# Batches 1 to 7 of an attention-and-mixer kernel in blocks of 512 columns across the batch borders

## The chip, the cores and the metric

The kernel runs on one core of a Trainium2 chip. Its engines are TensorE (PE, with the weight load, PEld, counted apart), VectorE (DVE), ScalarE (ACT), GpSimd (POOL) and SyncE (SP), which here issues the DMA transfers. The metric is the device time of one execution in microseconds (us); three executions of the kernel before took 809.54, 811.75 and 812.27 us.

## The reference

There are 8 batches of 576 tokens, 8 heads and 64 dimensions per head. Attention runs within chunks of 64 tokens; then a mixer runs over tokens and over channels:

```python
scores = scale * np.matmul(q_c, k_c.transpose(0, 1, 2, 4, 3))      # chunks of 64
attn = softmax(scores); out = np.matmul(attn, v_c)                 # x: (8, 576, 512)
xt = x.transpose(0, 2, 1)
h = np.maximum(xt @ w_tok1, 0.0) @ w_tok2                          # 576 -> 256 -> 576
u = x + h.transpose(0, 2, 1)
h2 = np.maximum(u @ w_ch1, 0.0) @ w_ch2                            # 512 -> 1536 -> 512
return (u + h2).astype(np.float32)
```

All four mixer weights come in as float64 words. The token mixer (tok1, tok2) mixes the 576 tokens of one batch with each other; the channel mixer (ch1, ch2) treats every token alone, so for it the tokens of all batches are one row of 4608 columns.

## The kernel before

**Precision.** Each operand is split in a high part in fp32r and the rest in fp32r (names in `h` and `l`: `uh`, `ul`, `gh`, `gl`, `rh`, `rl`, `xh`, `xl`), and each product is three matmuls (the table `THREE`: high times high, low weight times high, high weight times low). In batch 0 tok1 and the plain products of tok2 work on fp32 instead.

**Weights.** A weight arrives as raw words (`raw_t` for the token mixer, `raw_c` for the channel mixer, L139, issued from SP in an order that the program gives). ACT (L156, L157), DVE (L160, L166, L173, L181) make fp32 of it, ACT (L225) its high part, DVE (L231) its low part. The 24 items of the channel mixer alternate: `c1_f` and `c2_f` for each f from 0 to 11. `AHEAD` says how many items ahead the load is issued; `convert(n)` takes n operations off the list of conversions, and the tables `FIRST_FILL`, `PREPARE`, `END_FILL` and `STEP_FILL` say how many at which place.

**Attention.** The 72 chunks of two batches make nine tiles of 128 tokens; the fifth is shared by both batches ("stack"). A tile goes through scores (QK, L270 and L309), maximum (L282), subtraction (L285), exponential (L289), a transpose through memory (DVE writes `blocks`, L332; SP writes `far`, L337, and reads it back as `pf`, L343; ACT copies `pt`, L360), the product with v (PV, L321 and L379), the scaling that gives `x` (L400), its split (`xh` by ACT L417, `xl` by POOL L418) and a second way through `far` into `xt`, the transposed x (L343). The shared tile goes through `xc` (SP, L429) and `xr` (ACT, L433) as well.

**Mixer.** Batch by batch. tok1 (L476) has two groups of 14 matmuls with 512 columns. ACT and DVE make `rh` (L493) and `rl` (L494) of them. tok2 (L514) works in two halves of 288 columns and four output parts m: eight groups of six matmuls of 288 columns, in the banks `ps_acc`; DVE adds `xt` (`u`, L519), ACT writes `uh` (L524), POOL or DVE writes `ul` (L525). Then, for each half, twelve steps f: ch1 (L535, 12 matmuls of 288 columns into one of two banks `ps_c1`), ACT writes `gh` (L544), DVE writes `gl` (L545), and one step later ch2 (L575, 12 matmuls into the four banks `ps_acc`). After the last step DVE and POOL add u (L582, L584) and SP stores 288 columns at a time. In batch 0, where the weights are still being converted, both halves go through ch1 together (the second half's g is kept), and the second half's ch2 runs at the end, beside the attention of batch 1. tok1 of the next batch stands round the last ch2 but one, and 28 attention steps are put at chosen steps f.

**What sets the order.** PE, ACT and DVE follow the written order until the first half of batch 0 has its u. After that the order of each engine comes from a scheduler that works with its own estimate of time; from batch 1 on, PE again follows the written order. Each engine works through its list in order, and SP does too: a DMA that waits for its data holds all that stand behind it.

## Time and profile before

| | |
|---|---|
| times of three executions, us | 809.54, 811.75, 812.27 (median 811.75) |
| span of the profiled execution, us | 808.2 |
| median less that span, us | 3.55 |
| PE busy in the span | 787.4 us (97%) |
| DVE, ACT, POOL busy | 378.0, 240.7, 118.5 us |
| mean granted TensorE clock | 0.992 |

The page gives the span of the profiled execution, from the first to the last instruction, and no time of its own; the timed executions have a median that is 3.55 us longer, which lies around the span. The profile has four stages: the start (0 to 43 us, attention of batch 0 and the first weights), batch 0 (43 to 152 us), batches 1 to 7 (152 to 804 us) and the last stores.

A row of the timeline has the start, the duration, the engine, the line, the operation and the tiles; "x2" stands for two equal instructions in a row, whose duration runs from the first start to the last end. Matmuls are pipelined, so the cost of one is read from start to start. "[2.49 <-ACT xh L417]" is idle time before the row and what ended it.

### The profile page before, as it was taken

Reading aid. Unit: us, or ns where it says so; the run is one execution under the profiler, and the core shown is the slowest. Engines: PE = TensorE matmul, PEld = TensorE weight load, DVE = VectorE, ACT = ScalarE, POOL = GpSimd, SP = SyncE. Lnnn points to the kernel's source line nnn. Section 1 sums busy time; section 2 is a strip of 40 time slices with the busy share of each in tenths; the row PEclk is TensorE's granted clock in tenths of the full one; section 3 lists DMA queues with packets and bytes.
Section 4 is the critical chain, followed back from the end, with each engine's and each line's share of the span. In section 5 each row is a group of like instructions: output and inputs, shape, how many; then the busy total and the mean of one; then the engine's idle time right before and its main releaser. Section 6 shows DMA issues by size and latency. Waiting matters only on the chain.

```text
span 808.2 us, 17939 instructions
## 1 busy us (share of the span) xinstructions
PE 787.4 (97%) x7556; PEld 752.1 (93%) x7556; DVE 378.0 (47%) x799; ACT 240.7 (30%) x496; POOL 118.5 (15%) x137
## 2 busy tenths in 40 slices
...
PEclk8999999999999999999999999999999999999999
...
GB/s 349 406 190 105 119 79 96 135 122 141 148 112 64 92 122 107 56 79 125 141 151 58 64 115 140 88 70 93 131 145 89 76 88 101 67 30 1 1 30 30
DMA packets 69985, 87.96 MB, mean 109 GB/s; under 512 B 8016, under 2 KB 48208, under 8 KB 69904
## 3 DMA queue, kind: packets, MB, share of 16 engines
...
q14 instruction: 22, 0.18, 0.1%
HBM read 59.92 MB, written 25.95 MB: 106 GB/s over the span
## 4 chain that ended last, share of the span: by engine, by line
PE 85%; DVE 8%; DMA 3%; ACT 2%; issue 1%; SPq 0%; ACTq 0%; DVEq 0%
PE acc L575 36%; PE ps_c L535 33%; PE ps_t L476 6%; PE ps_t L514 6%; PE ps_sv L309 2%; PE ps_sv L321 2%; DVE wtop L173 1%; DVE wtop L181 1%; DMA xc<-x 1%; DVE kept_c L231 1%; DVE wtop L160 1%; DMA raw_t<-in_w 1%; DMA pf<-far 1%; DVE wtop L166 1%; PE sum L485 0%
## 5 line engine op out<-in xcount | busy, mean ns | idle before, releaser
L535 PE MATMUL ps_c<-uh,kept_c 128*128 128x288 f32 x1536 | 310.8, 295 | 3.4 <-ACT xt L447 1.9
L575 PE MATMUL acc<-gh,kept_c 128*128 128x288 f32 x1536 | 311.9, 299 | 1.6 <-ACT kept_c L225 1.1
L535 PEld LDWEIGHTS ps_c<-uh,kept_c 128*128 128x128 f32 x1536 | 245.8, 188 | 4.8 <-ACT xt L447 2.1
L575 PEld LDWEIGHTS acc<-gh,kept_c 128*128 128x128 f32 x1536 | 244.2, 188 | 6.4 <-ACT kept_c L225 1.8
L535 PE MATMUL ps_c<-ul,kept_c 128*128 128x288 f32 x768 | 226.6, 295 | 0.0
L545 DVE SCALAR_TENSOR_TENSOR gl<-ps_c,gh 128x288 fp32r<-128x288 f32 x180 | 81.4, 452 | 310.1 <-ACT gh L544 309.9
L575 PE MATMUL acc<-gl,kept_c 128*128 128x288 f32 x768 | 219.5, 295 | 0.0
L544 ACT ACTIVATE gh<-ps_c 128x288 fp32r<-128x288 f32 x180 | 74.1, 411 | 317.1 <-PE ps_c L535 316.6
L535 PEld LDWEIGHTS ps_c<-ul,kept_c 128*128 128x128 f32 x768 | 144.2, 188 | 0.1
L575 PEld LDWEIGHTS acc<-gl,kept_c 128*128 128x128 f32 x768 | 142.9, 189 | 0.1
L418 POOL TENSOR_TENSOR xl<-x,xh 128x512 fp32r<-128x512 f32 x28 | 38.3, 1366 | 413.0 <-ACT xh L417 413.0
L584 POOL TENSOR_TENSOR o<-o,ul 128x288 f32<-128x288 f32 x56 | 44.1, 813 | 192.7 <-DVE o L582 191.1
L514 PE MATMUL ps_t<-kept_t,rh 128*128 128x288 f32 x224 | 44.7, 295 | 0.3 <-ACT rh L493 0.3
L289 ACT ACTIVATE pr<-pr 128x512 f32<-128x512 f32 x36 | 22.7, 632 | 61.6 <-DVE pr L285 59.9
L582 DVE TENSOR_TENSOR o<-acc,uh 128x288 f32<-128x288 f32 x56 | 22.7, 448 | 36.1 <-PE acc L575 31.5
L476 PE MATMUL ps_t<-xh,kept_t 128*128 128x512 f32 x112 | 36.0, 405 | 2.5 <-ACT xh L417 2.5
L524 ACT CAST uh<-u 128x288 fp32r<-128x288 f32 x64 | 27.1, 433 | 37.6 <-DVE u L519 37.6
L360 ACT COPY pt<-pf 128x512 f32<-128x512 f32 x31 | 19.2, 620 | 60.3 <-DMA pf<-far 60.3
L514 PEld LDWEIGHTS ps_t<-kept_t,rh 128*128 128x128 f32 x224 | 35.9, 188 | 1.0 <-ACT rh L493 1.0
L514 PE MATMUL ps_t<-kept_t,rl 128*128 128x288 f32 x112 | 33.2, 297 | 0.2 <-DVE rl L494 0.2
L519 DVE TENSOR_TENSOR u<-ps_t,xt 128x288 f32<-128x288 f32 x64 | 28.4, 452 | 9.8 <-PE ps_t L514 9.4
L525 POOL TENSOR_TENSOR ul<-u,uh 128x288 fp32r<-128x288 f32 x35 | 29.1, 848 | 10.0 <-ACT uh L524 9.5
...
## 6 DMA issues: line engine op xcount, KB each, us to landing
...
```

Source lines behind the costliest of these rows:

```text
L289: nc.scalar.activation(out=pr, in_=pr, func=AF.Exp, scale=1.0 / float(D) ** 0.5)
L418: nc.gpsimd.tensor_tensor(out=xl, in0=t["x"], in1=xh.bitcast(F32), op=ALU.subtract)
L476: nc.tensor.matmul(ps, lhsT=lhsT, rhs=rhs, start=(n == 0 and q == 0), stop=(n == len(mt) - 1 and q == len(terms) - 1),)
L514: nc.tensor.matmul(ps[:, :HALF], lhsT=lhsT[:, m * P:(m + 1) * P], rhs=rhs, start=(k == 0 and q == 0), stop=(k == NT1 - 1 and q == len(term ...
L519: nc.vector.tensor_tensor(out=u.rearrange("p (i c) -> p i c", c=BK), in0=ps[:, :HALF].rearrange("p (i c) -> p i c", c=BK), in1=xt[:, n * H ...
L524: nc.scalar.copy(out=uh[:, m], in_=u)
L525: return lambda engine: engine.tensor_tensor(out=ul[:, m], in0=u, in1=uh[:, m].bitcast(F32), op=ALU.subtract)
L535: nc.tensor.matmul(ps[:, :HALF], lhsT=weights["c1", f][:, wi, k * P:(k + 1) * P], rhs=u[ui][:, k], start=(k == 0 and q == 0), stop=(k == N ...
L544: nc.scalar.activation(out=gh, in_=ps[:, :HALF], func=AF.Relu)
L545: nc.vector.scalar_tensor_tensor(out=gl, in0=ps[:, :HALF], scalar=0.0, in1=gh.bitcast(F32), op0=ALU.max, op1=ALU.subtract)
L575: nc.tensor.matmul(accs[e], lhsT=weights["c2", f][:, wi, e * P:(e + 1) * P], rhs=g[gi], start=(f == 0 and q == 0), stop=(f == NFC - 1 and ...
L584: nc.gpsimd.tensor_tensor(out=o, in0=o, in1=u[1][:, e].bitcast(F32), op=ALU.add)
```

## The change

Batch 0 stays in two halves of 288 columns. The 4032 tokens of batches 1 to 7 become one row of columns, cut in seven blocks of 512 and one of 448. tok2 of a block is made in pieces cut at the batch borders: 512; 64+448; 128+384; 192+320; 256+256; 320+192; 384+128; 448. Each piece has four parts m of six matmuls. The function that writes it is `block_tok2`; its four groups go to the two banks `ps_c1` in turn and the fourth to the bank of the attention (`ps_at`), not to `ps_acc`. `turn(k + 1)` places them between ch2 of f = 10 and ch2 of f = 11 of the block before. tok1 of batch k + 2 (both groups) stands after ch1 of f = 11, ahead of ch2 of f = 10. The attention steps stand at f in `SLOTS`, every second step, and the first one is moved into batch 0.

`xt` is a buffer per block (two of them) beside one for batch 0; u, uh and ul are tiles of one part m; `ul` is written by POOL for m = 0 and 2 and by DVE for m = 1 and 3. The tok2 weights come in two items of 576 columns and not four of 288. `AHEAD` goes from 6 to 2 and the tables of fills are new. v is loaded with its column of ones for the first nine tiles alone. The output is laid out as 4 x 128 x 4608 and stored in pieces of 512 columns.

```diff
-AHEAD = 6
+N = 512
+BLOCKS = [(k * N, min(N, (B - 1) * S - k * N)) for k in range(-(-(B - 1) * S // N))]
+SLOTS = {0: (1, 3, 5, 7, 9), 1: (2, 4, 6, 8), 2: (1, 3, 5, 7, 9)}
+UL_ON_VECTOR = {1, 3}
+AHEAD = 2
...
-END_FILL = (4, 3, 1)
-STEP_FILL = (5, 5)
+END_FILL = (4, 3, 1, 1, 1, 3, 2)
+STEP_FILL = (4, 5, 5, 5, 5, 5, 5, 4, 5, 5, 5, 5, 5, 5, 5, 5, 5, 6, 5, 5, 5, 6, 5, 5)
...
-    plan += [(("t2", k, n), w2_in, k * S + n * HALF, HALF) for n in range(2) for k in range(NT1)]
+    plan += [(("t2", k), w2_in, k * S, S) for k in range(NT1)]
...
+    def block_tok2(k, rs, m, dst, ps):
+        uh, ul = dst
+        cols = slice(m * P, (m + 1) * P)
+        base, width = BLOCKS[k]
+        at = 0
+        while at < width:
+            b, lo = divmod(base + at, S)
+            n = min(S - lo, width - at)
+            terms = [
+                (rs[b + 1][t][ri], weights["t2", t][:, wi, lo:lo + n]) for t in range(NT1) for wi, ri in THREE
+            ]
+            for q, (lhsT, rhs) in enumerate(terms):
+                nc.tensor.matmul(
+                    ps[:, at:at + n], lhsT=lhsT[:, cols], rhs=rhs,
+                    start=(q == 0), stop=(q == len(terms) - 1),
+                )
+            at += n
+        u = pool.tile([P, N], F32, tag="o", name="u", bufs=8)[:, :width]
...
+            in1=block_x(k)[:, :width // BK, m], op=ALU.add,
+        )
+        nc.scalar.copy(out=uh[m], in_=u)
+        (nc.vector if m in UL_ON_VECTOR else nc.gpsimd).tensor_tensor(
+            out=ul[m], in0=u, in1=uh[m].bitcast(F32), op=ALU.subtract
+        )
...
+    def turn(k, rs):
+        u = block_u(BLOCKS[k][1])
+        for m in range(NDT):
+            if m < 3:
+                ps = ps_c1.tile([P, 512], F32, tag="c1", name="ps_t2")
+            else:
+                ps = ps_at.tile([P, 2, 512], F32, tag="at", name="ps_t2")[:, 0]
+            block_tok2(k, rs, m, u, ps)
+        return u
...
+        if f == NFC - 1:
+            after.close()
+            by_hand.enter_context(tc.manual_schedule(engines={nc.tensor.engine}))
+            u = turn(0, rs)
+        ch2(HALF, HALF, us[1], f, g, accs)
+        extras(2 * NFC + f)
+        if f == FIRST_QK:
+            attention(0)
+
+    done = 1
+    for k, (at, width) in enumerate(BLOCKS):
+        mixes = k + 2 if k + 2 < B else None
+        steps = SLOTS[0] if k == 0 else SLOTS[1 + (len(batch_tiles(mixes)) == 5)] if mixes else ()
...
+        for f in range(NFC):
+            g = ch1(u, f, width=width)
+            if f in steps:
+                attention(done)
+                done += 1
+            end = f == NFC - 1
+            if end and mixes:
+                rs[mixes] = [tok1(mixes, m) for m in range(NT1)]
+            if pend is not None:
+                ch2(*pend)
+            pend = (S + at, width, u, f, g, accs)
+            if end and k + 1 < len(BLOCKS):
+                u = turn(k + 1, rs)
+            if end:
+                ch2(*pend)
```

The order on PE at the border of batches 1 and 2, before: the last tok1 matmul (`stack` is the shared tile, `half_low` its masked low weights), ch2 of f = 11, then tok2 in groups of 288 columns, and ch1 of f = 0 at the end.

```order
L476 MATMUL ps_t1_3454<-stack_3290,half_low0_2053 128x512
L575 MATMUL acc_2979<-gh_3419,kept_c2_11_1687 128x288 x2
L575 MATMUL acc_2979<-gl_3420,kept_c2_11_1687 128x288
...
L514 MATMUL ps_t2_3503<-kept_t2_0_0_2076,rh_3438 128x288 x2
L514 MATMUL ps_t2_3503<-kept_t2_0_0_2076,rl_3439 128x288
L514 MATMUL ps_t2_3503<-kept_t2_1_0_2098,rh_3469 128x288 x2
L514 MATMUL ps_t2_3503<-kept_t2_1_0_2098,rl_3470 128x288
...
L535 MATMUL ps_c1_3597<-uh_3501,kept_c1_0_648 128x288 x2
```

The same place in the changed kernel, at the end of block 0, with its own line numbers (L504 is tok1, L572 tok2, L594 ch1, L636 ch2):

```order
L504 MATMUL ps_t1_2982<-stack_2888,half_low_2068 128x512
L636 MATMUL acc_2372<-gh_2930,kept_c2_10_1555 128x512 x2
...
L572 MATMUL ps_t2_3021<-kept_t2_0_2074,rh_2146 128x64 x2
L572 MATMUL ps_t2_3021<-kept_t2_0_2074,rl_2147 128x64
L572 MATMUL ps_t2_3021<-kept_t2_1_2112,rh_2181 128x64 x2
L572 MATMUL ps_t2_3021<-kept_t2_1_2112,rl_2182 128x64
L572 MATMUL ps_t2_3021<-kept_t2_0_2074,rh_2978 128x448 x2
...
L636 MATMUL acc_2372<-gh_2959,kept_c2_11_1609 128x512 x2
...
L594 MATMUL ps_c1_3122<-uh_3013,kept_c1_0_575 128x512 x2
```

ch1 and ch2 are 512 wide, tok2 moved ahead of ch2 of f = 11, and each of its groups here is a piece of 64 columns (the rest of batch 1) and one of 448 (batch 2).

The order on PE at the end of batch 0, before: the last ch2 rows, the last PV (L379), then the share of the last attention tile (`xh_1991`) in tok1, then tok2.

```order
L575 MATMUL acc_1897<-gl_2165,kept_c2_11_1687 128x288
L379 MATMUL ps_v_1953<-v_1597,pt_1951 64x65 x16
L476 MATMUL ps_t1_2145<-xh_1991,kept_t1_2_2_2028 128x512 x2
L476 MATMUL ps_t1_2180<-xh_1991,kept_t1_2_2_2028 128x512 x2
L476 MATMUL ps_t1_2145<-xl_1992,kept_t1_2_2_2028 128x512
L476 MATMUL ps_t1_2180<-xl_1992,kept_t1_2_2_2028 128x512
L514 MATMUL ps_t2_2239<-kept_t2_0_0_2076,rh_2160 128x288 x2
```

And in the changed kernel (L397 is PV, L327 QK, `xh_1951` the last tile's):

```order
L397 MATMUL ps_v_1913<-v_1572,pt_1911 64x65 x16
L636 MATMUL acc_1865<-gh_2115,kept_c2_10_1555 128x288 x2
...
L327 MATMUL ps_sv_1995<-qk_1766 64x64 x16
L504 MATMUL ps_t1_2131<-xh_1951,kept_t1_2_2_1992 128x512 x2
L504 MATMUL ps_t1_2166<-xh_1951,kept_t1_2_2_1992 128x512 x2
L504 MATMUL ps_t1_2131<-xl_1952,kept_t1_2_2_1992 128x512
L504 MATMUL ps_t1_2166<-xl_1952,kept_t1_2_2_1992 128x512
L572 MATMUL ps_t2_2195<-kept_t2_0_2074,rh_2146 128x512 x2
...
L636 MATMUL acc_1863<-gh_2150,kept_c2_11_1609 128x288 x2
```

Six matmuls of ch2 of f = 10 and the QK of the next tile now stand between the last PV and the tok1 rows that need it, and ch2 of f = 11 stands behind the four tok2 groups of block 0.

The order of the loads on SP in the first part of batch 0, before: `xc` behind the raws up to `c1_10`.

```order
L139 DMA raw_c2_7_117<-in_wc2 128x1024
L139 DMA raw_c1_9_113<-in_wc1 128x1024
L139 DMA raw_c2_8_109<-in_wc2 128x1024
L139 DMA raw_c1_10_105<-in_wc1 128x1024
L429 DMA xc_1158<-x_663 64x512
...
L139 DMA raw_c2_9_101<-in_wc2 128x1024
L139 DMA raw_c1_11_97<-in_wc1 128x1024
L139 DMA raw_c2_10_93<-in_wc2 128x1024
```

And in the changed kernel (L140 raws, L447 `xc`, L355 `far`, L361 its way back):

```order
L140 DMA raw_c2_7_117<-in_wc2 128x1024
L447 DMA xc_1131<-x_637 64x512
...
L140 DMA raw_c1_9_113<-in_wc1 128x1024
L140 DMA raw_c2_8_109<-in_wc2 128x1024
L140 DMA raw_c1_10_105<-in_wc1 128x1024
...
L140 DMA raw_c1_11_97<-in_wc1 128x1024
L355 DMA far_1422<-blocks_1420 128x512
L361 DMA pf_1424<-far_1422 32x4x128 x4
L140 DMA raw_c2_10_93<-in_wc2 128x1024
L140 DMA raw_c2_11_89<-in_wc2 128x1024
```

`xc` moved ahead of three raws, and the last two raws moved behind the reading back of the second tile's transpose.

On DVE, before, c2_10 is clamped (L160) side by side with c1_11 soon after the second tile's transpose (`blocks_1446`):

```order
L332 STREAM_TRANSPOSE blocks_1446<-pr_1399 128x4x4x32
L181 ISA wtop_1319<-wtop_1319,low_1320 128x1024
L160 TENSOR_SCALAR wtop_1432<-wtop_1432 128x512
...
L160 TENSOR_SCALAR wtop_1515<-wtop_1515 128x512
L181 ISA wtop_1432<-wtop_1432,low_1433 128x1024
L160 TENSOR_SCALAR wtop_1569<-wtop_1569 128x512
```

In the changed kernel (L166 is the clamp, L187 the add, L237 the low part; `wtop_1490` is c2_10):

```order
L350 STREAM_TRANSPOSE blocks_1420<-pr_1342 128x4x4x32
L187 ISA wtop_1292<-wtop_1292,low_1293 128x1024
L237 TENSOR_TENSOR kept_c1_9_1340<-wtop_1223,kept_c1_9_1340 128x512
...
L187 ISA wtop_1445<-wtop_1445,low_1446 128x1024
L237 TENSOR_TENSOR kept_c2_9_1457<-wtop_1406,kept_c2_9_1457 128x512
L411 TENSOR_SCALAR zi_1523<-ps_v_1506 128x8
L166 TENSOR_SCALAR wtop_1490<-wtop_1490 128x512
```

The clamp of c2_10 moved from the 14th to the 19th place behind the transpose, with 17 conversions and gl and one small `zi` (L411) between.

More of the change, by code (lines that the diff above doesn't have):

```diff
@@ L152, in words_scalar @@
         st = raws[i][1]
-        tag, bufs = (f"wt{n}", token) if i < token else ("wt", 4)
-        tops[i] = pool.tile([P, n], F32, tag=tag, name="wtop", bufs=bufs)
-        lows[i] = pool.tile([P, DM], I32, tag="low", name="low", bufs=3)[:, :n]
+        if i < token:
+            if "t" not in tops:
+                tops["t"] = pool.tile([P, sum(p[3] for p in plan[:token])], F32, tag="wtt", name="wtt", bufs=1)
+            lo = sum(p[3] for p in plan[:i])
+            tops[i] = tops["t"][:, lo:lo + n]
+        else:
+            tops[i] = pool.tile([P, n], F32, tag="wt", name="wtop", bufs=4)
+        lows[i] = pool.tile([P, max(n, DM)], I32, tag="low" if n < S else "low_t", name="low", bufs=3)[:, :n]
         nc.scalar.activation(out=tops[i], in_=st[:, :, 1].bitcast(F32), func=AF.Abs)
@@ L442, in attn_x @@
                 continue
+            if b:
+                first, end = ((b - 1) * S + j * P + r for r in (0, rows.stop - rows.start))
+                while first < end:
+                    k, at = divmod(first, N)
+                    n = min(end - first, N - at)
+                    part = slice(rows.start, rows.start + n)
+                    far_in(tiles[t]["x"], block_x(k)[:, at // BK:(at + n) // BK], part)
+                    rows = slice(part.stop, rows.stop)
+                    first += n
+                continue
             dst = xt[:, 4 * j:4 * j + (rows.stop - rows.start) // BK]
@@ L666, in attention_mixer_kernel @@
     second = batch_tiles(1)
+    order = [t for b in range(2, B) for t in batch_tiles(b)]
     attn_load(second[0])
```

210 lines of the change are left out of this document (95 added, 115 removed).

## The prediction

> **What bounds the kernel now.** I read the page first, then busy time by stretch, then the timelines of the two stretches where something is lost. The page, with the clock in tenths over the span and the chain that ended last:
>
> ```profile
> span 808.2 us, 17939 instructions
> PE 787.4 (97%) x7556; PEld 752.1 (93%) x7556; DVE 378.0 (47%) x799; ACT 240.7 (30%) x496; POOL 118.5 (15%) x137
> PEclk8999999999999999999999999999999999999999
> PE 85%; DVE 8%; DMA 3%; ACT 2%; issue 1%; SPq 0%; ACTq 0%; DVEq 0%
> ```
>
> PE is busy for 97% of the span. Busy time by stretch (us, number of instructions in brackets, then granted clock, DMA share, GB/s) says where the rest is:
>
> ```profile
> 43.00:60.00 17.00, 16.00 (x110) 13.35 (x110) 14.83 (x33) 10.91 (x21) 0.00 (x0) 0.90 0.45 164
> 60.00:80.00 20.00, 20.00 (x173) 19.31 (x172) 20.00 (x43) 15.20 (x30) 0.00 (x0) 1.00 0.31 106
> 80.00:100.00 20.00, 19.29 (x166) 18.19 (x165) 20.00 (x40) 14.43 (x28) 2.99 (x1) 1.00 0.37 120
> 100.00:120.00 20.00, 18.84 (x191) 17.76 (x190) 17.27 (x36) 9.87 (x21) 4.72 (x5) 1.00 0.21 68
> 143.80:152.00 8.20, 5.27 (x35) 3.64 (x27) 4.29 (x10) 1.73 (x4) 4.13 (x5) 0.79 0.28 92
> 230.00:700.00 470.00, 470.00 (x4611) 458.63 (x4610) 192.36 (x400) 116.34 (x242) 76.66 (x84) 1.00 0.31 98
> ```
>
> From 230 to 700 us PE never idles and has its full clock, so in batches 1 to 7 only fewer or shorter matmuls save time. From 60 to 100 DVE, converting weights, is full too: there PE and DVE bind together.
>
> **The wide matmuls.** The price of one, on PE's timeline:
>
> ```profile
> 700.48 0.42 PE L535 MATMUL ps_c<-uh,kept_c 128*128 128x288 f32 x2
> ...
> 710.02 0.42 PE L535 MATMUL ps_c<-uh,kept_c 128*128 128x288 f32 x2
> ...
> 711.60 0.39 PE L476 MATMUL ps_t<-stack,kept_t 128*128 128x512 f32 x1
> ...
> 714.86 0.42 PE L575 MATMUL acc<-gh,kept_c 128*128 128x288 f32 x2
> ```
>
> From 700.48 to 710.02 lie three steps of 24, so 9.54 / 72 = 132.5 ns for 288 columns. From 711.60 to 714.86 lie the 14 matmuls of one tok1 group: 232.9 ns for 512. The slope is 100.4 / 224 = 0.448 ns a column, and 3.4 ns are left that every matmul pays. ch1 and ch2 of batches 1 to 7 are 7 x 576 = 4032 matmuls of 288 now (534.2 us) and become 2016 of 512 (469.5) and 288 of 448 (204.2 each, 58.8): 528.3, a gain of 5.9. If ch2, which changes its bank every three matmuls, costs 1 ns more than tok1 at 512, 1.2 of that goes. I take **-5.0**, with 3 and 8 as the ends, which the last digit of the four rows allows. The number of columns stays, so nothing larger is to be had.
>
> The Trainium skill, "TensorE: Matmul & The Clock Gate", section "Back-to-back issue gap", gives N/2.4 + 2.5 ns for an isolated matmul, and 131 ns for N = 512 in a sustained stream. By the first the gain would be 1728 x 2.5 = 4.3 us; the second would make the stage 200 us shorter, and the 232.9 ns above, from a sustained stream, contradict it.
>
> **tok2 in pieces.** Batches 1 to 7 have 24 x 14 = 336 tok2 matmuls before and after, of the same 96768 columns. But 24 now have 64 columns, 48 have 128 and 48 have 192, which by the slope take 32, 61 and 89 ns. A weight load of 128 columns goes with each, and no row of 128-column weights in fp32r shows less than 132 ns. The nearest rows:
>
> ```profile
> 23.16 0.60 PE L351 MATMUL ps_x<-ident,x 128*128 128x128 f32 x4
> 23.60 0.60 PE L351 MATMUL ps_t<-ident,pr 128*128 128x128 f32 x4
> ...
> 266.78 0.69 PE L309 MATMUL ps_sv<-qk 64*64 64x64 f32 x32
> 267.29 0.65 PE L321 MATMUL ps_sv<-v,pt 64*64 64x64 f32 x32
> ```
>
> L351 takes 0.44 / 4 = 110 ns with 128 columns of fp32 and a load of 128. QK takes 0.51 / 32 = 16 ns in tiles of a quarter of the array, 64 ns for each quarter. A floor of 110 costs 24 x 78 + 48 x 49 + 48 x 21 ns = 5.2 us, one of 64 costs 0.9, none costs 0. I take **+2.0**, nearer to the small tiles, since L351's fp32 is not the type here.
>
> The Trainium skill, "TensorE: Matmul & The Clock Gate", section "LDWEIGHTS (loading the stationary operand)", has P/1.2 ns for P columns, 107 for 128. Were that the floor, the pieces would cost 4.9 us and the time would be 2.9 longer than my sum; no row before shows it.
>
> **The end of batch 0.** PE, DVE, ACT and SP there:
>
> ```profile
> 143.34 0.70 PE L379 MATMUL ps_v<-v,pt 64*64 64x65 f32 x32
> 146.53 2.08 PE L476 MATMUL ps_t<-xh,kept_t 128*128 128x512 f32 x4 [2.49 <-ACT xh L417]
> 148.40 1.06 PE L476 MATMUL ps_t<-xl,kept_t 128*128 128x512 f32 x2
> 149.72 0.55 PE L514 MATMUL ps_t<-kept_t,rh 128*128 128x288 f32 x2 [0.26 <-ACT rh L493]
> 150.44 0.40 PE L514 MATMUL ps_t<-kept_t,rl 128*128 128x288 f32 x1 [0.18 <-DVE rl L494]
> ...
> 151.28 0.43 PE L514 MATMUL ps_t<-kept_t,rh 128*128 128x288 f32 x2
> ...
> 143.11 1.55 DVE L582 TENSOR_TENSOR o<-acc,uh 128x288 f32<-128x288 f32 x4 [4.66 <-issue]
> ...
> 145.07 0.69 DVE L400 TENSOR_TENSOR x<-ps_v,zi 128x512 f32<-128x512 f32 x1
> ...
> 148.57 1.73 SPq L343 DMA_DIRECT2D xt<-far  x4
> ```
>
> The last PV ends at 144.04 (call that T); DVE is still at the four o adds, so x starts at T + 1.0, and PE waits 2.49 us. The matmuls behind the wait run at about half speed (the stretch's clock is 0.79). Up to 151.28 pass 7.24 us with 6 x 0.233 + 6 x 0.1325 = 2.2 of work: 5.0 lost. After the change the o adds come later, x starts at T + 0.5, and 0.8 us of ch2 and 0.5 of QK stand behind PV. xh's matmuls follow x's start by 1.46 as now, so at T + 2.0: a wait of 0.7. xl (POOL, 1.37 us a piece) comes another 0.5 late. rh and rl behind the shorter tok1 cost some 0.7. Then two tok2 groups of 1.4 run to T + 7.4, and the third needs the bank `ps_c1` of the first, which u (DVE) has to leave; u needs xt of the last tile. That lands now 6.5 us after x is ready (145.76 to 150.30 + 2.0), so at T + 7.7, and u takes 0.7: a new wait of 1.0. Loss after: 2.9. **-2.1**, with 0 and 5 as the ends. ch2 of f = 11 then gives 1.6 us for the last uh and ul.
>
> **Attention and its transfers.** One wait of batches 1 to 7 goes, and the transfer of the shared tile moves:
>
> ```profile
> PE ps_sv L321 <- ACT pt L360: 0.5, 1, 0.5
> PE ps_c L535 <- ACT uh L524: 1.0, 1, 1.0
> ...
> 276.63 0.62 ACT L360 COPY pt<-pf 128x512 f32<-128x512 f32 x1 [1.63 <-DMA pf<-far]
> ...
> 41.35 9.72 DMA xc<-x
> ...
> 51.10 0.62 ACT L433 CAST xr<-xc 64x512 fp32r<-64x512 f32 x1 [2.92 <-DMA xc<-x]
> ```
>
> From QK (266.78) to the end of pt is 10.5 us; steps will be two f apart, 48 x 0.233 = 11.2, with 1.1 of attention in them 12.3. So the 0.5 goes: **-0.5**. xc is issued at 41.35 and lands 9.72 us later behind the raws; ACT waits for it 2.92 us with uh queued behind, and PE 1.0 for uh. With three raws fewer ahead of it that ends: **-1.0**.
>
> The last two raws speak against the change. They will be issued behind the pf of the second tile:
>
> ```profile
> 94.71 0.33 SPq L337 DMA_DIRECT2D far<-blocks  x1
> 96.77 1.75 SPq L343 DMA_DIRECT2D pf<-far  x4
> DMA to landing us min/median/max: 5.1/5.7/6.9
> ...
> L231 DVE TENSOR_TENSOR kept_c<-wtop,kept_c 128x512 fp32r<-128x512 f32 x12 | 8.1, 674 | 0.0
> L545 DVE SCALAR_TENSOR_TENSOR gl<-ps_c,gh 128x288 fp32r<-128x288 f32 x7 | 3.1, 444 | 0.0
> ```
>
> The third row is that of raws (L139) issued from 60 to 100 us; the last two have DVE's mean ns of one in about that stretch. From the transpose to the end of the pf issues are 3.8 us, and with 0.4 for its own issue and 5.7 c2_10 lands after 9.9. In the new order DVE has 17 other conversions and gl between that transpose and c2_10's first operation: 11 of 0.67 us (sign, add, low part) and 6 of 0.44 (clamp, shift, gl), 10.0 us, of which ACT needs 0.7 for itself: 0.6 late, 1.8 at the slowest landing. ACT would stand at the raw with gh behind it. **+0.5**.
>
> At the start AHEAD, the fills and the wider tok2 items shift some 2 us of DVE work ahead of the first ch1 and take about as much out of the stretch where DVE is full: 0, with 2 each way. In a step of 5.6 us, gh and gl at 512 columns take what these do:
>
> ```profile
> L494 DVE SCALAR_TENSOR_TENSOR rl<-ps_t,rh 128x512 fp32r<-128x512 f32 x14 | 9.5, 686 | 21.1 <-ACT rh L493 21.1
> L493 ACT ACTIVATE rh<-ps_t 128x512 fp32r<-128x512 f32 x14 | 8.3, 597 | 45.3 <-PE ps_t L476 45.3
> ...
> 804.26 0.46 DVE o L582
> ```
>
> 0.6 and 0.7 us lie beside 2.8 us of ch2, so they cost nothing; were they bare, it would be 1.3 a step. The last add on 448 columns and its store: **+0.3**.
>
> **Sum.** -5.0 + 2.0 - 2.1 - 0.5 - 1.0 + 0.5 + 0.3 = -5.8, a span of 802.4. The median lies 3.55 above the span, so 806.0 against 811.75.
>
> **Rivals.** *Batch 0 gains more.* The stretches from 43 to 120 lose 1.0 + 0.7 + 1.2 in idle and 1.7 by the clock of 0.90; if the new fills end most of it (3.5 more), the end of batch 0 loses half of what I say (1.5) and the pieces have no floor (2.0), the time is 799. For it: DVE runs full from 60 us on, and what it has done earlier is no longer in the way; against: the conversions are as many as before, and PE idles little. *The pieces and turns eat the gain.* With a floor of 110 ns (+3.2) and 0.15 us of waiting at each of seven turns (+1.0) it is 810.2, within the noise of no change. *The attention chain becomes the bound, slower.* A step has 12.3 us, the chain 10.5 today. gh and gl in front of its six DVE and ACT operations, u and ul at the turns and SP's stores of 512 columns ahead of `far` can lengthen it; above 12.3 PE waits at PV in each of 28 steps. From 12.6 on (0.3 x 28 = 8.4) the change is slower; at 12.65, 806.0 + 9.8 = 815.8. Against it: DVE is busy for 192 of 470 us, and 1.8 us are in hand. *A long stream of 512 columns runs faster than the tok1 group*: every 10 ns would be 20 us. The group's 14 in a row at 232.9 show no such trend. The 131 ns of the Trainium skill ("TensorE: Matmul & The Clock Gate", "Back-to-back issue gap") would make it some 600 us.
>
> **How the numbers follow.** Chances: the forecast (802 to 809) 0.45, more in batch 0 (795 to 802) 0.22, gain eaten (809.3 to 814.2) 0.20, chain or another new wait (above 814.2) 0.12, the faster stream 0.01. A measurement of this kernel tells 0.3% from no change, 809.3 to 814.2. So faster 0.45 + 0.22 + 0.01 = 0.68, same 0.20, slower 0.12. The range from 797 to 813.5 leaves out some of the first rival and the slower one.
>
> **What would show it.** ch1 and ch2 at 232 to 234 ns from start to start in the new trace; the pieces of 64 and 128 columns at 32 and 61 ns (no floor) or near 110; PE's wait for xh at the end of batch 0 under 1 us and one for u or xt before the third tok2 group; no PE wait for pt; ACT's wait for xc gone, one for the last raws below 2 us. I am wrong if PE shows waits at the turns or at PV in each step, or if the first 150 us move by more than 5 us.

## The result and the profile after

The changed kernel takes 803.83 us (median of 803.06, 803.81, 804.65 and 803.84) against 812.01 for the kernel before in the same runs (809.54 to 812.36): a ratio of 0.9906, interval 0.9891 to 0.9921. That is 8.2 us faster; forecast were 806.0, and 797 to 813.5 as the range.

The profiled execution after took 803.06 us, 1.76 more than its span of 801.3. The page of the changed kernel, the same lines as before:

```profile
span 801.3 us, 14067 instructions
PE 781.5 (98%) x5828; PEld 650.2 (81%) x5828; DVE 364.9 (46%) x664; ACT 223.2 (28%) x394; POOL 108.7 (14%) x94
PEclk7999999999999999999999999999999999999999
PE 81%; DMA 9%; DVE 7%; issue 1%; SPq 1%; ACT 0%; POOL 0%; ACTq 0%; DVEq 0%
```

Busy time by stretch of the changed kernel (us, instructions in brackets, granted clock, DMA share, GB/s):

```profile
43.00:60.00 17.00, 14.36 (x105) 12.46 (x103) 16.74 (x38) 12.63 (x25) 0.00 (x0) 0.90 0.18 61
60.00:80.00 20.00, 19.44 (x172) 18.98 (x171) 19.22 (x41) 15.38 (x31) 0.00 (x0) 1.00 0.32 106
80.00:100.00 20.00, 20.00 (x179) 19.77 (x178) 20.00 (x41) 13.85 (x27) 2.49 (x1) 1.00 0.42 141
143.80:152.00 8.20, 6.76 (x54) 4.30 (x47) 5.93 (x11) 2.57 (x6) 1.98 (x2) 1.00 0.47 142
230.00:700.00 470.00, 470.00 (x3409) 386.59 (x3409) 186.01 (x311) 103.50 (x171) 74.37 (x56) 1.00 0.30 97
```

From 230 to 700 us PE is still busy all the time, now with 3409 matmuls and not 4611. PE's waits from 43 to 160 us in the changed kernel (us in total, times, longest); behind 160 us the view is empty, so no wait at any turn and none for `pt` in batches 1 to 7:

```profile
PE ps_v L397 <- ACT pt L378: 3.4, 3, 1.3
PE ps_c L594 <- ACT xt L475: 2.6, 1, 2.6
PE ps_t L572 <- DVE rl L522: 0.8, 1, 0.8
...
PE ps_t L572 <- ACT rh L521: 0.5, 1, 0.5
...
```

**Where the 6.9 us of span went.** From the start of the first tok2 of batch 1's tokens to the start of the last matmul (before 149.72 and 803.86, after 146.77 and 797.31) pass 654.14 us before and 650.55 after, with ch2 of batch 0's f = 11 (1.58 us) in the latter alone. I added up every matmul there from its start to the next one's:

| us, start to start | before | after | difference |
|---|---|---|---|
| ch1 and ch2 of batches 1 to 7 | 539.5 | 529.8 | -9.7 |
| tok2 | 45.1 | 51.2 | +6.1 |
| QK and PV | 30.4 | 29.0 | -1.4 |
| tok1 | 39.2 | 39.0 | -0.2 |
| ch2 of batch 0, f = 11 | | 1.6 | +1.6 |

Ahead of this stage the change wins 2.95 (149.72 to 146.77), behind it 0.4. The 2.95 is one execution against one: in four experiments below that have the same code up to the first tok2 (the halves, the half loads, the turns last, four matmuls a group) it starts at 145.23 to 148.33. From the last PV to the first tok2 pass 5.3 us in each of them, as here, against 6.4 before.

The wide matmuls on PE's timeline of the changed kernel, two pairs of rows, each one step of 24 matmuls apart:

```profile
300.48 0.61 PE L594 MATMUL ps_c<-uh,kept_c 128*128 128x512 f32 x2
306.05 0.63 PE L594 MATMUL ps_c<-uh,kept_c 128*128 128x512 f32 x2
...
719.87 0.62 PE L594 MATMUL ps_c<-uh,kept_c 128*128 128x512 f32 x2
725.40 0.63 PE L594 MATMUL ps_c<-uh,kept_c 128*128 128x512 f32 x2
```

5.57 / 24 = 232.1 and 5.53 / 24 = 230.4 ns for 512 columns. In the last block 448 take 204.5 in the mean.

The pieces of 64, 128 and 192 columns in the changed kernel, each with the row that follows the six matmuls of its group, and the two rows of the 448 columns behind the 64:

```profile
232.31 0.30 PE L572 MATMUL ps_t<-kept_t,rh 128*128 128x64 f32 x2
232.45 0.28 PE L572 MATMUL ps_t<-kept_t,rl 128*128 128x64 f32 x1
232.56 0.39 PE L572 MATMUL ps_t<-kept_t,rh 128*128 128x64 f32 x2
232.89 0.65 PE L572 MATMUL ps_t<-kept_t,rh 128*128 128x448 f32 x2
233.39 0.36 PE L572 MATMUL ps_t<-kept_t,rl 128*128 128x448 f32 x1
...
318.09 0.33 PE L572 MATMUL ps_t<-kept_t,rh 128*128 128x128 f32 x2
318.71 0.56 PE L572 MATMUL ps_t<-kept_t,rh 128*128 128x384 f32 x2
...
404.53 0.36 PE L572 MATMUL ps_t<-kept_t,rh 128*128 128x192 f32 x2
405.18 0.48 PE L572 MATMUL ps_t<-kept_t,rh 128*128 128x320 f32 x2
```

A group of six takes 0.58, 0.62 and 0.65 us, nearly the same for 64, 128 and 192 columns. Between the third and the fourth matmul of the 64 (232.45 to 232.56) lie 110 ns. Only the first of a group is shorter, since its load ran beside the wide matmul ahead of it; the wide piece behind pays some back (0.50 us for its first two).

The end of batch 0 in the changed kernel: PE from the last PV to the last group of tok2, and ch2 of f = 11 behind:

```profile
141.49 0.70 PE L397 MATMUL ps_v<-v,pt 64*64 64x65 f32 x32 [1.33 <-ACT pt L378]
...
144.19 1.19 PE L504 MATMUL ps_t<-xh,kept_t 128*128 128x512 f32 x4
146.77 0.73 PE L572 MATMUL ps_t<-kept_t,rh 128*128 128x512 f32 x2 [0.52 <-ACT rh L521]
149.28 0.50 PE L572 MATMUL ps_t<-kept_t,rl 128*128 128x512 f32 x1 [0.77 <-DVE rl L522]
153.78 0.42 PE L636 MATMUL acc<-gh,kept_c 128*128 128x288 f32 x2
```

The wait for xh (2.49 us before) is gone. PV ends at 142.12, where ch2 goes on. From there to 153.78 pass 11.66 us with 6 x 0.1325 of ch2, 0.5 of QK and 30 x 0.232 of tok1 and tok2, 8.3 of work: 3.4 lost, against 5.0 before. About half of it is in the waits shown, the rest in matmuls that run slower behind them (146.77 to 149.28).

### The profile page after: what moved, and what is told of

Same layout as the page of the kernel before. It is cut to its first block, busy times and chain, and to the rows that moved or that the text cites. A ratio compares the mean times of both kernels' runs of the same rounds, so it can differ in the third digit from the quotient of the medians.

```text
span 801.3 us, 14067 instructions
## 1 busy us (share of the span) xinstructions
PE 781.5 (98%) x5828; PEld 650.2 (81%) x5828; DVE 364.9 (46%) x664; ACT 223.2 (28%) x394; POOL 108.7 (14%) x94
## 4 chain that ended last, share of the span: by engine, by line
PE 81%; DMA 9%; DVE 7%; issue 1%; SPq 1%; ACT 0%; POOL 0%; ACTq 0%; DVEq 0%
PE acc L636 33%; PE ps_c L594 33%; PE ps_t L572 6%; PE ps_t L504 5%; DMA raw_c<-in_wc 3%; DMA far<-blocks 2%; PE ps_sv L327 2%; DMA raw_t<-in_w 2%; PE ps_sv L339 2%; DMA pf<-far 1%; DMA xc<-x 1%; DVE wtop L187 1%; DVE wtop L179 1%; DVE kept_c L237 1%; SPq L361 1%
## 5 line engine op out<-in xcount | busy, mean ns | idle before, releaser
L636 PE MATMUL acc<-gh,kept_c 128*128 128x512 f32 (+2 forms) x960 | 273.2, 374 | 0.0
L594 PE MATMUL ps_c<-uh,kept_c 128*128 128x512 f32 (+1 forms) x768 | 238.3, 391 | 0.0
L606 DVE SCALAR_TENSOR_TENSOR gl<-ps_c,gh 128x512 fp32r<-128x512 f32 (+2 forms) x108 | 70.9, 657 | 319.3 <-ACT gh L605 319.3
L636 PEld LDWEIGHTS acc<-gh,kept_c 128*128 128x128 f32 x960 | 170.3, 188 | 29.8
L636 PE MATMUL acc<-gl,kept_c 128*128 128x512 f32 (+2 forms) x480 | 170.7, 370 | 0.0
L594 PEld LDWEIGHTS ps_c<-uh,kept_c 128*128 128x128 f32 x768 | 144.1, 188 | 31.0
L594 PE MATMUL ps_c<-ul,kept_c 128*128 128x512 f32 (+1 forms) x384 | 149.8, 390 | 0.0
L605 ACT ACTIVATE gh<-ps_c 128x512 fp32r<-128x512 f32 (+2 forms) x108 | 61.6, 570 | 291.7 <-PE ps_c L594 291.6
L636 PEld LDWEIGHTS acc<-gl,kept_c 128*128 128x128 f32 x480 | 88.0, 188 | 15.0
L436 POOL TENSOR_TENSOR xl<-x,xh 128x512 fp32r<-128x512 f32 x28 | 37.5, 1338 | 375.4 <-ACT xh L435 364.4
L594 PEld LDWEIGHTS ps_c<-ul,kept_c 128*128 128x128 f32 x384 | 72.1, 188 | 15.7
L572 PE MATMUL ps_t<-kept_t,rh 128*128 128x448 f32 (+7 forms) x224 | 48.6, 311 | 0.5 <-ACT rh L521 0.5
L594 PE MATMUL ps_c<-both,kept_c 128*128 128x288 f32 x288 | 44.1, 304 | 3.2 <-ACT xt L475 2.6
L594 PEld LDWEIGHTS ps_c<-both,kept_c 128*128 128x128 f32 x288 | 40.4, 193 | 4.1 <-ACT xt L475 2.9
L572 PEld LDWEIGHTS ps_t<-kept_t,rh 128*128 128x128 f32 x224 | 37.3, 189 | 2.6 <-ACT rh L521 0.9
L572 PE MATMUL ps_t<-kept_t,rl 128*128 128x448 f32 (+7 forms) x112 | 34.9, 313 | 0.8 <-DVE rl L522 0.8
```

The lines of the kernel that those rows point to most:

```text
L436: nc.gpsimd.tensor_tensor(out=xl, in0=t["x"], in1=xh.bitcast(F32), op=ALU.subtract)
L572: nc.tensor.matmul(ps[:, at:at + n], lhsT=lhsT[:, cols], rhs=rhs, start=(q == 0), stop=(q == len(terms) - 1),)
L594: nc.tensor.matmul(ps[:, :width], lhsT=weights["c1", f][:, wi, k * P:(k + 1) * P], rhs=u[ui][k], start=(k == 0 and q == 0), stop=(k == NDT ...
L605: nc.scalar.activation(out=gh, in_=ps[:, :width], func=AF.Relu)
L606: nc.vector.scalar_tensor_tensor(out=gl, in0=ps[:, :width], scalar=0.0, in1=gh.bitcast(F32), op0=ALU.max, op1=ALU.subtract)
L636: nc.tensor.matmul(accs[e], lhsT=weights["c2", f][:, wi, e * P:(e + 1) * P], rhs=g[gi], start=(f == 0 and q == 0), stop=(f == NFC - 1 and ...
```

## The experiments

All of them start from the changed kernel; a ratio is against the kernel before in the same set of runs. Its median lay between 810.7 and 812.0 from set to set, so a microsecond between two versions says little.

**Is the gain the price of a matmul?** Every wide matmul of ch1 and ch2 but the first of its bank is made in two halves of 256:

```diff
-                nc.tensor.matmul(
-                    ps[:, :width], lhsT=..., rhs=u[ui][k],
-                    start=(k == 0 and q == 0), stop=(k == NDT - 1 and q == 2),
+                for lo, hi in HALVES(width, k == 0 and q == 0): nc.tensor.matmul(
+                    ps[:, lo:hi], lhsT=..., rhs=u[ui][k][:, lo:hi],
+                    start=(k == 0 and q == 0), stop=(k == NDT - 1 and q == 2 and hi == width),
```

> The changed kernel with the ch1 and ch2 matmuls of the seven 512-column blocks issued as two matmuls of 256 columns each (all but the first of each accumulation): 1904 more matmuls, the same columns, nothing else. The forecast's theory, 3.4 ns for every matmul beside its columns, expects 1904 x 3.4 = 6.5 us more, 810.3 us. The rival, that a wide matmul is cheaper than its tok1 row said and the fixed part larger (two of 256 at 118.2 ns against one of 512 at 230.9 in the changed kernel's trace, 5.5 ns), expects 10.5 us more, 814.3 us. If neither a fixed part nor anything else counts, 803.8 us.

It took 817.89 us (816.72 to 818.44), ratio 1.0086 [1.0061, 1.0112]: 14.1 more than the changed kernel for 1904 more matmuls, 7.4 ns each, above both expectations. Its waits up to 160 us are those of the changed kernel to within 0.1 us. One step on its PE timeline, 47 matmuls, one of them whole:

```profile
733.10 0.64 PE L594 MATMUL ps_c<-uh,kept_c 128*128 128x512 f32 x3
738.82 0.64 PE L594 MATMUL ps_c<-uh,kept_c 128*128 128x512 f32 x3
```

(5.72 - 0.23) / 46 = 119.3 ns for 256 columns, so two of them cost 7.6 more than one of 231. Fewer matmuls for the same columns are what the change gains in this stage, and a matmul more at 256 columns costs over twice the 3.4 ns that I had read from two widths. It brings a weight load of its own; the run doesn't tell the two apart.

**What holds the narrow pieces up?** Four of the six matmuls of a piece below 256 columns load 64 weight columns and not 128 (so half of the output rows lack these four products):

```diff
+ROWS = lambda n, q: P if n >= 256 or q in (0, 3 * NT1 - 1) else P // 2
...
-                    ps[:, at:at + n], lhsT=lhsT[:, cols], rhs=rhs,
+                    ps[:ROWS(n, q), at:at + n], lhsT=lhsT[:, cols.start:cols.start + ROWS(n, q)], rhs=rhs,
```

> The changed kernel with 64 instead of 128 weight columns in four of the six matmuls of each tok2 group in the pieces of 64, 128 and 192 columns; half of their output rows lack these four products. In the changed kernel such a matmul takes about 113 ns whatever its width. If the weight load is that floor, these 80 matmuls fall to about 57, 61 and 89 ns: 16 x 56 + 32 x 52 + 32 x 24 ns = 3.3 us less, 800.5 us. If the floor lies in the issue of a matmul, it stays at 113 ns and at 803.8 us.

803.94 us (801.81 to 804.84), ratio 0.9908 [0.9882, 0.9934]: the median doesn't move. But tok2's sum falls from 51.17 to 48.05 us, 3.1 less. The first piece of 64 columns on PE's timeline, then a row from PE's waits of the same kernel:

```profile
230.85 0.22 PE L572 MATMUL ps_t<-kept_t,rl 128*64 128x64 f32 x1
230.91 0.28 PE L572 MATMUL ps_t<-kept_t,rh 128*64 128x64 f32 x2
231.03 0.28 PE L572 MATMUL ps_t<-kept_t,rl 128*128 128x64 f32 x1
...
PE ps_sv L339 <- ACT pt L378: 1.8, 1, 1.8
```

From 230.85 to 231.03 lie three matmuls with 64 weight columns: 60 ns each, where 128 took about 111. The moving columns are the same, so the load of the weights is the floor. In this execution a wait for `pt` at 382 us is new: 3.1 won, 1.8 lost, and its span is 1.3 shorter (800.0). The same step in the changed kernel, first on ACT's timeline, then on PE's:

```profile
382.68 0.62 ACT L378 COPY pt<-pf 128x512 f32<-128x512 f32 x1 [4.47 <-DMA pf<-far]
...
383.53 0.65 PE L339 MATMUL ps_sv<-v,pt 64*64 64x64 f32 x32
```

`pt` is ready at 383.30 and PV starts at 383.53: only 0.2 us in hand. In the experiment the four `pf` transfers took 4.8 us from the first issue to `pt` where these took 3.5. The Trainium skill, "TensorE: Matmul & The Clock Gate", section "LDWEIGHTS (loading the stationary operand)", gives P/1.2 ns for P columns, 107 and 53; the measured 111 and 60 lie 4 to 7 ns above it.

**Where the turn stands.** tok2 of the next block behind ch2 of f = 11, not ahead of it:

```diff
-            if end and k + 1 < len(BLOCKS):
-                u = turn(k + 1, rs)
             if end:
                 ch2(*pend)
+            if end and k + 1 < len(BLOCKS):
+                u = turn(k + 1, rs)
```

> The changed kernel with the tok2 of blocks 1 to 7 behind the last ch2 step of the block before instead of ahead of it; the number of matmuls is the same. The forecast's theory: the chain u, uh, ul behind the last tok2 group takes 0.7 + 0.6 + 0.7 = 2.0 us, and the nine ch1 matmuls that don't need it take 2.1, so at most 0.3 us of waiting at each of seven turns: 803.8 to 806 us. The rival, that only the ch2 step between tok2 and ch1 keeps these stages free of waits: 1 us or more at each turn, 811 us or more, with PE waits for uh or ul at ch1.

807.12 us (804.95 to 810.84, ten executions), ratio 0.9957 [0.994, 0.9974]: 3.3 more. New in PE's waits is a row for VectorE's `ul`, beside 0.6 us for GpSimd's:

```profile
PE ps_c L594 <- DVE ul L584: 0.7, 1, 0.7
```

Together they are 1.3 of it. From ch1 of f = 11 to the last ch1 matmul of the next block's f = 0, start to start, the seven turns add up to 161.6 us here and 158.9 in the changed kernel: 2.7 more. Three turns have 0.65, 0.61 and 1.21 of that, the other four at most 0.12 each. So ch2 of f = 11 does hide the last `u`, `uh` and `ul`, and without it a turn costs 0.4 us in the mean. To eat the gain of 8.2 it would have to be 1.2.

The same for block 0 alone (`turn(0, rs)` behind ch2 of batch 0):

> The changed kernel with the tok2 of block 0 behind the last ch2 step of batch 0 and not ahead of it (blocks 1 to 7 as they are). That step's 1.6 us then cover the waits for rh and rl (0.5 and 0.8 us in the changed kernel): 1.3 us less, 802.5 us, if u of the last part is ready in time. The rival: without the step between tok2 and ch1, ACT's pt, which now stands ahead of the third uh and waits for its transfer, holds uh, and TensorE waits 2 us or more at the first ch1 of block 0: 804.5 us or more.

809.85 us (807.93 to 812.78, ten executions), ratio 0.9981 [0.9962, 1.0]: 6.0 more, as the rival said. ACT's timeline has the cause:

```profile
157.28 0.62 ACT L378 COPY pt<-pf 128x512 f32<-128x512 f32 x1 [4.75 <-DMA pf<-far]
157.81 0.61 ACT L583 CAST uh<-u 128x512 fp32r<-128x512 f32 x1
```

The scheduler put `pt` ahead of the third `uh`; ACT stood 4.75 us at the transfer and PE 3.1 us for that `uh`. Behind that wait the granted clock is 0.50 from 160 to 165 us, and a matmul of 512 columns takes 427 ns (160.41 to 164.25 for nine). With the wait, the first two ch1 steps take 12.3 us, against 5.7 in the changed kernel. The waits for rh and rl ahead of it stayed at 0.5 and 0.8.

**Loads and attention in batch 0.** `AHEAD` back to 6:

```diff
-AHEAD = 2
+AHEAD = 6
```

> The changed kernel with AHEAD 6 as before and not 2, nothing else: the raw weights are asked for four items earlier, so xc stands behind four more of them and the last two raws no longer stand behind the second tile's pf. The forecast's terms expect ACT to wait for xc about as before (2 to 4 us, some 1 us of it on TensorE: +1.0) and not for the last raw (0.69 us in the changed kernel: -0.5), 804.3 us in all. The rival, that the loads' order is what makes batch 0 shorter: +3 us or more, 807 us.

804.0 us (803.79 to 806.79), ratio 0.9929 [0.9901, 0.9956]. The total can't be told from the changed kernel's; the waits can. ACT's, then PE's:

```profile
ACT xr L451 <- DMA xc<-x: 2.8, 1, 2.8
...
PE ps_c L594 <- ACT both L548: 1.6, 1, 1.6
```

Both come back (2.92 and 1.0 before), and ACT's wait for the late raw, 0.7 us in the changed kernel, is gone. So the order of the loads is the cause of these waits. What they cost is not shown: the first tok2 starts at 147.95, within the 145.23 to 148.33 of the same code, and PV's waits for `pt` in batch 0 fall from 3.4 us to 0.3 at the same time.

The attention steps of batch 0 where they were:

```diff
-STARTS = ((8, 9, 11, 12), (12, 14, 16, 17), (18, 19, 19, 22), (23, 23, 26, 27))
+STARTS = ((8, 9, 11, 12), (13, 14, 16, 17), (18, 19, 21, 22), (23, 24, 26, 27))
```

> The changed kernel with the attention jobs of batch 1 at the places they had before (STARTS (13, 14, 16, 17), (18, 19, 21, 22), (23, 24, 26, 27) for the second to fourth tile), nothing else. The forecast ascribed the gain at the end of batch 0 to the ch2 matmuls placed behind the last PV and not to these places: then the last PV stays at 141 to 142 us, tok2 of block 0 begins within 0.5 us of 146.8, and the time is 803.8 us, within 1. The rival, that the earlier places are what brought the last PV from 143.3 to 141.5 us: PV 1.5 to 2 us later, 805.5 us.

805.45 us (803.45 to 807.16), ratio 0.9937 [0.9914, 0.996]. The last PV starts at 140.36 and the first tok2 at 145.70, not later than in the changed kernel and within the spread of its own code (139.94 to 143.04 for the PV). So nothing shows that the new places shorten the end of batch 0; the median's 1.6 us are within the spread of these executions.

**The start.** The first ch1 begins 3.1 us later than before (45.87 against 42.78), and I had it at 0 with 2 each way; in five experiments with the same start it begins at 44.60 to 46.21. Two other sets of fills, first one with three conversions taken from the last place of `FIRST_FILL` to the first of `END_FILL`:

```diff
-FIRST_FILL = (3, 3, 5, 4, 4)
+FIRST_FILL = (3, 3, 5, 4, 1)
...
-END_FILL = (4, 3, 1, 1, 1, 3, 2)
+END_FILL = (7, 3, 1, 1, 1, 3, 2)
```

> The changed kernel with three conversion operations of the first stage moved behind the copy of the fifth tile's pt (FIRST_FILL's last entry 4 to 1, END_FILL's first 4 to 7), so that ACT does not stand at the first high weight part with pt behind it (2.2 us of PE waiting at 31.75 us). Theory A: the start is on the path, and ch1, which begins 3.1 us later than in the kernel before, begins 1 to 3 us earlier and so does everything behind: 801 to 803 us. Theory B: VectorE is full from 60 to 100 us, so the conversions set when batch 0 ends, and a later or earlier first ch1 is lost in that: 803.8 us, within 0.5.

816.71 us (814.2 to 818.08), ratio 1.0067 [1.0044, 1.0089]; neither expectation holds. PV came 1.3 us earlier, but DVE then stood at a conversion with x queued behind it, and PE waited 2.93 us for x:

```profile
33.23 0.69 DVE L237 TENSOR_TENSOR kept_c<-wtop,kept_c 128x512 fp32r<-128x512 f32 x1 [1.13 <-ACT kept_c L231]
```

The first ch1 started at 48.58, and from there on the orders on ACT and DVE were others. The second version leaves the conversions to the first step of ch1:

```diff
-FIRST_FILL = (3, 3, 5, 4, 4)
-PREPARE = (0, 1, 2, 1, 2)
+FIRST_FILL = (3, 3, 5, 4, 1)
+PREPARE = (0, 1, 2, 1, 1)
...
-END_FILL = (4, 3, 1, 1, 1, 3, 2)
-STEP_FILL = (4, 5, 5, ...)
+END_FILL = (3, 3, 1, 1, 1, 1, 2)
+STEP_FILL = (10, 5, 5, ...)
```

> The changed kernel with the conversions of the start put later, and such that the fifth tile's x waits for none of them: FIRST_FILL's last entry 4 to 1, PREPARE's last 2 to 1, END_FILL (3, 3, 1, 1, 1, 1, 2), STEP_FILL's first 4 to 10; the same operations in all. The first ch1 should begin at 41 to 43 us, not 45.9. Theory A, the start is on the path up to the end of batch 0: 3 to 4 us less, 800 us. Theory B, VectorE's conversions set the end of batch 0 whenever ch1 begins: 803.8 us, within 1.

808.39 us (806.9 to 811.75, ten executions), ratio 0.998 [0.9964, 0.9997]. The first and the last ch1 step of batch 0 on PE's timeline, of this kernel and then of the changed one:

```profile
42.17 1.73 PE L594 MATMUL ps_c<-both,kept_c 128*128 128x288 f32 x11 [1.88 <-ACT xt L475]
109.26 3.46 PE L594 MATMUL ps_c<-both,kept_c 128*128 128x288 f32 x24
```

```profile
45.87 3.01 PE L594 MATMUL ps_c<-both,kept_c 128*128 128x288 f32 x11 [2.64 <-ACT xt L475]
108.83 3.35 PE L594 MATMUL ps_c<-both,kept_c 128*128 128x288 f32 x24
```

3.7 us earlier at the first step are 0.4 later at the twelfth, which starts at 107.63 to 109.61 in the five experiments with the start unchanged. Between them DVE has hardly a gap (in the changed kernel it is busy for 55.96 of the 57 us from 43 to 100), and its work doesn't get less. That is the likely reason why the changed kernel's later start costs it nothing by the twelfth step, too. The first tok2 of the second version starts at 145.43, within the spread of the same code, and from there to the last matmul it takes 6.1 us longer than the changed kernel. The scheduler's order on ACT has `pt` ahead of the last two `uh` here too (waits of 1.1 for uh and 0.6 for ul), and the step at 385 us waits 1.8 for `pt`; these are 3.5 of it, the rest is open.

**Does DVE set the pace of batch 0?** If so, ten of its low parts on GpSimd, which is idle from 43 to 80 us, must help:

```diff
-        nc.vector.tensor_tensor(
+        (nc.gpsimd if key[0] == "c2" and key[1] < 10 else nc.vector).tensor_tensor(
```

> The changed kernel with the low weight parts of c2_0 to c2_9 made by GpSimd and not by VectorE: ten of VectorE's 0.68 us operations between 45 and 110 us go, 6.8 us, and GpSimd, idle up to 85 us, gets ten of about 1.4 us. If VectorE's conversions set the end of batch 0 (ch1 of f = 11 stayed at 108 to 109 us when the first ch1 came 3.7 us earlier), that ch1 begins 3 to 6 us earlier and the kernel takes 798 to 801 us. The rival, that TensorE itself is full there (19.4 and 20.0 us of 20) and the attention of batch 1 sets the end: 803.8 us, within 1.

816.63 us (813.92 to 820.6), ratio 1.0071 [1.0049, 1.0092]: 12.8 slower, and both expectations are wrong. The conversions on GpSimd from 40 to 120 us in this kernel, then VectorE's from 60 to 100 (count, busy time, mean ns of one):

```profile
L237 POOL TENSOR_TENSOR kept_c<-wtop,kept_c 128x512 fp32r<-128x512 f32 x9 | 20.1, 2239 | 47.8 <-ACT kept_c L231 47.8
...
L237 DVE TENSOR_TENSOR kept_c<-wtop,kept_c 128x512 fp32r<-128x512 f32 x7 | 7.3, 1043 | 0.0
L172 DVE TENSOR_SCALAR wtop<-wtop 128x512 int32<-128x512 int32 x11 | 7.1, 658 | 0.0
```

A subtraction of this size takes GpSimd 1.34 us in the changed kernel (L436, 28 of them) and 2.24 here; VectorE's two operations take 677 and 417 ns there and 1043 and 658 here. Both engines slow each other. Row by row it is one or the other: the subtraction at 86.20 us takes 1.28, and VectorE's L172 beside it 1.26; the one at 54.20 takes 3.04, and VectorE's operations beside it keep their durations. ch1 of f = 11 starts 9.0 us later than in the changed kernel (117.81); how that adds up from the single operations is open. With the second start on top:

> The kernel with the earlier start (808.39 us) and the ten low parts on GpSimd as well. If VectorE's conversions were what swallowed the earlier start, the 3.7 us now reach ch1 of f = 11 (about 105 us) and the time falls by 4 us or more below that of the earlier start alone, 804 us or less. The rival: the waits of that kernel behind 140 us (uh, ul, pt: 3.5 us) come from the scheduler's other order of the turn at the end of batch 0 and stay: 807 us or more.

810.99 us (808.99 to 814.45, ten executions), ratio 1.0008 [0.9994, 1.0022]. GpSimd's timeline and all its conversions (ns: least, median, most):

```profile
70.13 12.79 POOL L237 TENSOR_TENSOR kept_c<-wtop,kept_c 128x512 fp32r<-128x512 f32 x2 [2.69 <-ACT kept_c L231]
...
L237 POOL TENSOR_TENSOR kept_c<-wtop,kept_c x10: 1292/1660/11106, 38.7 to 106.7; 128x512 fp32r<-128x512 f32 x10
```

One subtraction took 11.1 us, while VectorE ran from 70.2 to 82 us without a gap and at its usual durations (busy for 20.00 of the 20 us from 60 to 80); PE waited 5.7 us for it. So whether a free DVE would quicken batch 0 stays untried, since this way of freeing it costs more than it frees. That DVE sets the pace there is argued from its missing gaps, not shown.

**A version with four matmuls a narrow group.** In pieces up to 128 columns, the high and the low weights are laid side by side as one moving operand, so a group needs four weight loads and not six; DVE adds the two halves:

```diff
+            if n <= P:
+                slot = m % (N // (2 * n)) * 2 * n
+                pair = spare[:, slot:slot + 2 * n]
+                for t in range(NT1):
+                    w2 = weights["t2", t][:, :, lo:lo + n]
+                    nc.tensor.matmul(
+                        pair.rearrange("p (w n) -> p w n", w=2), lhsT=rs[b + 1][t][0][:, cols], rhs=w2,
+                        start=(t == 0), stop=False,
+                    )
+                    nc.tensor.matmul(
+                        pair[:, :n], lhsT=rs[b + 1][t][1][:, cols], rhs=w2[:, 0],
+                        start=False, stop=(t == NT1 - 1),
+                    )
```

> The changed kernel with the tok2 pieces of 64 and 128 columns made in four matmuls a group and not six: the high and the low weights of the piece stand side by side as one moving operand of 128 or 256 columns, into the free half of the attention's bank, and VectorE adds the two halves. If the weight load of 113 ns is what such a matmul costs, twelve groups of 0.60 us fall to about 0.46 us: 1.7 us less, 802.1 us, with no wait at the turns. The rival: VectorE's two more additions a group come before uh and the next group's bank, and TensorE waits 0.3 us or more in each of the twelve groups, 804 us or more.

802.48 us (801.28 to 806.85), ratio 0.9904 [0.987, 0.9938]. The group of 64 columns takes 0.36 us and not 0.58 (PE's timeline, L573 the merged matmul, L588 the next piece); one new wait stands against it:

```profile
232.67 0.22 PE L573 MATMUL ps_t<-kept_t,rh 128*128 128x128 f32 x1
233.03 0.66 PE L588 MATMUL ps_t<-kept_t,rh 128*128 128x448 f32 x2
...
PE ps_t L588 <- DVE u L604: 1.2, 1, 1.2
```

tok2 adds up to 50.1 us, 1.1 less with that wait in it. It is the lowest median of all versions, though its interval holds the changed kernel's. Together with the conversions on GpSimd:

> The changed kernel with the ten low parts on GpSimd and the narrow tok2 pieces in four matmuls: the two effects should add, 1.3 us less than with GpSimd alone. If GpSimd brings nothing, 802.5 us as with the merged pieces alone.

812.75 us (810.51 to 817.21, ten executions), ratio 1.0027 [1.0007, 1.0048]: 3.9 below GpSimd's version alone, more than the pieces explain, with spreads of 6.7 us for both.

## Why the prediction was right, and where it was not

The likeliest case came: faster, by wide matmuls in a stage where PE never idles, with a gain at the end of batch 0. Several terms were wrong in size, and their errors cancelled: that the sum came within 1 us of the span is luck. In the profiled executions:

| term, us | forecast | measured |
|---|---|---|
| wide matmuls of ch1 and ch2 | -5.0 | -9.7 |
| tok2 in pieces | +2.0 | +5.4 |
| end of batch 0 | -2.1 | -1.6 |
| QK and PV, the wait for `pt` | -0.5 | -0.8 |
| batch 0 up to its last PV (xc -1.0, raws +0.5, start 0) | -0.5 | +0.5 |
| tok1 | 0 | -0.2 |
| last add and store | +0.3 | -0.4 |
| sum | -5.8 | -6.8 |

The span moved by 6.9; 0.1 is rounding of prices. For the second row, tok2 costs 44.35 before (336 x 132 ns) and 49.7 after (51.17 less 1.46 of waits and slow matmuls at block 0, which are in the third row). For the fourth, 0.5 of the 1.4 is the QK that moved into batch 0. For the fifth, the last PV starts 1.85 earlier, but 18 ch2 matmuls (2.4) that stood ahead of it now stand behind. This row is within the spread of the executions: by the last PV of the experiments with the same code (139.94 to 143.04) it could be -1.0 as well as +2.1.

**Wide matmuls: the size was off beyond the bound.** The step that failed is the price of 512 columns, taken from the 14 matmuls of one tok1 group (232.9 ns) and raised by 1 ns for ch2's banks. The 288 columns were priced rightly: 4032 x 132.5 = 534.2, and 539.5 less 5.3 for the attention steps is 534.2 (a ch1 ahead of QK takes 0.085 us more than another, a ch2 behind PV 0.106). After, 529.8 less 5.1 of attention and 58.9 for 288 matmuls of 204.5 leaves 465.8 / 2016 = 231.0 ns. 1.9 ns less in 2016 matmuls are 3.8 us, and the reserve of 1 ns was the rest. A difference of two prices, each read to a nanosecond, carried a stage with thousands of matmuls; a direct price was there only once a kernel with more matmuls had run. Nor is that price one for all widths: the change has 1728 matmuls fewer and wins 534.2 - 465.8 - 58.9 = 9.5 us by it, 5.5 ns for each, where the halves of 256 columns cost 7.4. Why is not shown. In other kernels of the experiments with the same wide matmuls they add up to 0.2 less to 1.8 more than here, so the -9.7 is uncertain by about as much. The 39 steps without attention or turn in the changed kernel's trace take 228.0 to 234.5 ns a matmul; why they differ stays open.

**Pieces: the high bound was the right one.** I took 2.0 between 0.9 and 5.2, since the row of 110 ns (L351) was of fp32. It was the price for fp32r too, by the load of 128 weight columns: the 24, 48 and 48 matmuls at 97, 103 and 108 ns (groups of 0.58, 0.62 and 0.65) less the 32, 61 and 89 of the slope are 4.5 us, and 0.9 is in the pieces behind them. The sentence on the P/1.2 of the Trainium skill had 4.9.

**End of batch 0: right in size, with one wait misplaced.** PE's wait for xh went; x and xh came earlier than T + 2.0 by so much that QK and ch2 covered them. The wait forecast at the third group, for u and `xt`, did not come; what came is 0.5 for rh and 0.77 for rl, close to the 0.7 in the working. rl was late because ACT does an exponential (146.61) between the two rh and DVE the transpose at 147.35.

**Transfers: the waits were right.** The wait for xc went and came back with `AHEAD` = 6, though no run shows the 1.0 and the 0.5 as time of the kernel; the last raw was late by 0.69 where 0.6 was forecast:

```profile
103.94 0.67 ACT L162 ACTIVATE wtop<-raw_c 128x512 f32<-128x512 f32 x1 [0.69 <-DMA raw_c<-in_wc]
```

**Start: outside its bounds, and swallowed.** The first ch1 is 3.1 late in this execution, not within 2 (1.8 to 3.4 in those with the same start); by the twelfth step nothing of it is left, and the second set of fills shows the same for an earlier start. In the term's +0.5 against -0.5 are also the three waits of PV for `pt` (3.4 in all), which I had not looked at: the attention steps of batch 0 are now closer to their transfers, and with the steps at their old places 1.3 are left.

**From the span to the time.** I added 3.55, the median less the span shown. But each profiled execution since lies 1.7 to 2.1 above its span. By that the profiled one before took about 810.0, near the low end of that kernel's executions. 802.4 + 1.8 would have been 804.2, and the measured median is 803.8: this step alone carries most of the forecast's error of 2.2.

**The rivals.** Batch 0 did not gain more: from 43 to 80 us PE idles more than before, from 80 to 100 less. Of the rival that eats the gain the floor came (3.4 us on top of the sum's 2.0, where it had 3.2), but the turns cost nothing where they stand. The chain of attention did not become the bound; the view of waits is empty behind 160 us. But I had 1.8 us in hand at every step, and at one of them it was 0.2: in four of the experiments that step waits 1.6 to 1.8 us. The slower rival had the place of the wait right and lacked 27 more such steps; where the wait came, the `pf` transfers were longer (4.8 us against 3.5 with half loads), and no run shows that gh, gl, u, ul or the stores lengthened the chain.
